# Attention of the last two chunks with keys by halves of a block, and their loads issued elsewhere

## The chip, the cores and the metric

The kernel runs on one core of a Trainium2 chip. The metric is the device time of one execution in microseconds. A core has five engines with a queue each, which work in order: TensorE (PE in the profile; its weight loads are PEld), VectorE (DVE), ScalarE (ACT), GpSimd (POOL) and SyncE (SP), which only issues DMAs here. GpSimd issues DMAs too (those that cast on the way), and all DMAs share 16 DMA engines.

## The reference, cut to what matters

Linear attention with decay, in blocks, and then a feed-forward layer with a PReLU (the reference walks in blocks of 64 positions; the kernel takes 128, which gives the same sums):

```python
q, k, v: (4, 8, 768, 64) fp32       # batch, heads, positions, head_dim
rel   = pos[:, None] - pos[None, :]
Dmask = where(rel >= 0, lam ** rel, 0)
for each block:
    intra = ((qb @ kb.T) * Dmask) @ vb
    inter = (qb * lam ** (pos + 1)) @ kv_state
    out   = intra + inter
    kv_state = lam ** block * kv_state + (kb * lam ** (block - 1 - pos)).T @ vb
x = out as (3072, 512)
h = x @ w_in                        # (512, 2048)
g = max(h, 0) + alpha * min(h, 0)
result = g @ w_out                  # (2048, 512), fp32
```

Within a block only the pairs with key position at or before the query position count; the mask is zero for the others.

## The kernel before

**Units and chunks.** The kernel takes blocks of L = 128 positions and windows of W = 256 (two blocks, numbered a = 0 and 1). A chunk c is one window of two of the four batch entries; there are six chunks, and the window of chunk c is c // 2. Each chunk is cut into four units by batch entry (bi) and half of the heads (hh), so unit n is chunk n // 4; units 16 to 23 are the last two chunks, 4 and 5. For these two chunks' window only the state of the first of its blocks is still needed, so their state products number 8 instead of 16.

**Positions.** Loads put neighbouring positions beside each other in one partition: partition p of a window holds positions 2p and 2p + 1 (e = 0 and 1), 128 numbers in a row, 512 bytes in HBM. Block a lies in partitions 64a to 64a + 63. A block's 128 keys are thus cut into even and odd ones.

**One unit's way.** `load` (L80) brings q, k and v in fp32, from SyncE by default; `load_v16` (L274) brings v from GpSimd and casts it on the way. `cast` (L263) makes fp16 copies of q and k in one tile `qk16`. `transposes` (L306) turns this tile by a DMA transpose from SyncE into `qkT`. `key_decayed` (L287) multiplies k by its decay (tile `kdec`) and `decayed` (L350) the turned q by its decay (tile `qdT`), nearly always on GpSimd. Then come the matmuls:

- `inter` (L368): decayed queries times state R, 128 columns, into the accumulator `acc`.
- `score_products` (L384): 16 matmuls of 64x64 quadrants, 128 query columns each, for two head pairs (hp) x two key halves (e) x four quadrants, into PSUM tile `s`.
- `masked` (L399): VectorE multiplies `s` (128 x 1024) by `dmask` into `sm`.
- `intra` (L409): 16 quadrant matmuls of values times `sm`, 128 columns each, into `acc`.
- `state_products` (L429): quadrant matmuls of `kdec` and values, 64 columns each, into the other half of `acc`; `states` (L455) folds them into R on VectorE.
- `attended` (L445): ScalarE copies `acc` into the chunk's `xT`.

`cluster(old, new)` (L478) issues these for two units at once, in this order on TensorE: inter of the old unit, scores of the new one, intra of the old one, state products of the new one. So the masked multiply of a unit has the time until the next cluster.

**The feed-forward layer.** `up(c, f, ...)` (L540) makes four matmuls of 512 columns into a bank of PSUM, ScalarE a negated relu `m` (L553) and VectorE the activation `g` (L560) from it. `down(c, t, part, ...)` (L567) multiplies four of the 16 tiles of `g` by `w_out`. For the chunks from 3 on, `down2` (L695) does this with sums of quarter matrices (`product`, L642; `g_sum`, L627; `weight_sum`, L615).

**The order.** Nothing is scheduled automatically. The order of each engine's queue is the order of the calls: up to L1037 a list written out by hand, and from L1045 a table `plan` for chunks 3, 4 and 5, whose entries are called at numbered steps of an alternation of up and down products. While chunk c's up products run, the clusters of chunk c + 1 come between. [...] The pools set how many tiles of a kind live at once: `raw` five, `qk16` four, `qkT` three, `v16` and `kdec` eight each (a unit's v is one tile).

## Time and profile before

| | us |
|---|---|
| median of 3 runs | 207.44 (207.35 to 207.44) |
| the profiled execution, its own time | 207.43 |
| its span, first to last instruction | 205.7 |
| TensorE busy | 200.0 (97%) |
| VectorE busy | 159.7 (78%) |
| ScalarE busy | 113.6 (55%) |
| GpSimd busy | 110.0 (53%) |

The span leaves out what lies around the program's instructions, 1.7 us here. The mean granted clock of TensorE is 0.997 of full speed. In the profile's rows, a timeline row gives start, duration, engine, line, operation, what it writes and reads, its shape and how many such instructions were merged; in brackets stands the idle time of that engine before it and what ended it. A row of a group gives the same by line and shape with the count, the busy time and the mean in ns.

### The profile page before, as it was taken

To read this page: it belongs to the slowest core of one execution; us is meant where nothing else is said; L and a number is where in the kernel's file an instruction comes from. 1 tells how busy PE (TensorE), PEld (TensorE's weight loads), DVE (VectorE), ACT (ScalarE), POOL (GpSimd) and SP (SyncE) were. 2 spreads that over 40 slices of the span, in tenths; PEclk is the share of its full clock that TensorE was granted. 3 is DMA by queue.
4 is the path that set the end of the run, shared out by engine and by line. 5 is a ranking of instruction groups with operands and counts; after the bars stand their busy time and mean duration, and the time that the engine had idled before them with its cause. 6 is when DMAs were issued, how large, how long until landed. Compare 5 with 4: busy or idle time off the path is not lost.

```text
span 205.7 us, 5585 instructions
## 1 busy us (share of the span) xinstructions
PE 200.0 (97%) x2271; PEld 122.7 (60%) x2271; DVE 159.7 (78%) x289; ACT 113.6 (55%) x210; POOL 110.0 (53%) x132
## 2 busy tenths in 40 slices
PE   7999999999999999999999999999999999999992
PEld 6976445556445455555555455466666666666882
DVE  6978879568888847899998887959999467675921
ACT  7885778144786217656776466653553544444320
POOL 8999794053577883295346995562094040552000
PEclk9999999999999999999999999999999999999998
DMA  5999999997999995999989974540001111011223
GB/s 165 278 197 234 245 259 207 233 285 238 222 266 233 207 292 131 242 155 137 175 100 269 203 201 78 77 102 21 33 0 54 64 42 51 2 51 54 81 73 105
DMA packets 58206, 31.18 MB, mean 152 GB/s; under 512 B 27124, under 2 KB 55940, under 8 KB 58180
## 3 DMA queue, kind: packets, MB, share of 16 engines
q1 hardware_dynamic: 42740, 21.12, 42.3%
q0 software_dynamic: 15136, 9.57, 29.3%
q8 instruction: 18, 0.29, 0.6%
q10 hardware_dynamic: 304, 0.13, 0.2%
q14 instruction: 8, 0.07, 0.1%
HBM read 27.27 MB, written 6.29 MB: 163 GB/s over the span
## 4 chain that ended last, share of the span: by engine, by line
PE 92%; DVE 2%; ACT 2%; issue 1%; ACTq 0%; DVEq 0%
PE h_ps L545 40%; PE o_ps L573 21%; PE o_ps L655 16%; PE s L391 4%; PE acc L416 3%; PE unread L152 2%; PE acc L375 2%; PE tpx L341 2%; PE acc L436 1%; DVE g L638 1%; ACT L180 1%; ACT m L553 1%; ACT xT L250 1%; DVE sm L402 1%; PE p L655 0%
## 5 line engine op out<-in xcount | busy, mean ns | idle before, releaser
L545 PE MATMUL h_ps<-xT,w_in_sb 128*128 128x512 f16 (+1 forms) x392 | 91.9, 375 | 0.2 <-DVE g L560 0.2
L560 DVE SCALAR_TENSOR_TENSOR g<-m,oma,h_ps 128x512 f16<-128x512 f32 (+1 forms) x98 | 71.1, 734 | 25.1 <-ACT m L553 22.0
L553 ACT ACTIVATE m<-h_ps 128x512 f32<-128x512 f32 (+1 forms) x98 | 57.3, 588 | 46.6 <-PE h_ps L545 40.4
L545 PEld LDWEIGHTS <-w_in_sb 128*128 128x128 f16 x392 | 37.5, 98 | 37.4 <-issue 0.4
L573 PE MATMUL o_ps<-w_out_sb,g 128*128 128x512 f16 x192 | 46.8, 380 | 0.0
L402 DVE TENSOR_TENSOR sm<-s,dmask 128x1024 f16<-128x1024 f32 x24 | 29.2, 1218 | 10.8 <-PE s L391 10.7
L655 PEld LDWEIGHTS <-g 128*128 128x128 f16 x296 | 28.2, 98 | 8.2
L638 POOL TENSOR_TENSOR s<-g 128x512 f16<-128x512 f16 x11 | 12.8, 1163 | 32.6 <-PE o_ps L655 16.7
L573 PEld LDWEIGHTS <-g 128*128 128x128 f16 x192 | 17.7, 98 | 19.4 <-DVE g L560 0.2
L250 ACT ACTIVATE xT<-acc 128x512 f16<-128x512 f32 x24 | 14.3, 597 | 24.3 <-PE acc L436 22.2
L355 POOL TENSOR_TENSOR qdT<-qkT,qdecay 128x512 f16<-128x512 f16 (+1 forms) x19 | 21.1, 1116 | 8.5 <-DMA qkT<-qk 5.3
L655 PE MATMUL o_ps<-w_out_sb,g 128*128 128x256 f16 x192 | 24.1, 273 | 0.0
L291 POOL TENSOR_TENSOR kdec<-kraw,kdecay 128x512 f16<-128x512 f32 x18 | 19.2, 1069 | 6.5 <-DVE g L560 5.4
L254 POOL CAST qk<-qraw 128x512 f16<-128x512 f32 x12 | 7.7, 645 | 18.2 <-DMA qraw<-in_q_dram 18.2
L465 DVE SCALAR_TENSOR_TENSOR R<-R,rdecay,acc 128x128 f16<-128x128 f16 x54 | 15.4, 338 | 0.0
L278 POOL DMA_DIRECT2D v<-in_v_dram x19 | 14.9, 790 | 0.4 <-issue 0.4
L638 POOL TENSOR_TENSOR g<-g 128x512 f16<-128x512 f16 x11 | 13.3, 1206 | 0.9
L687 ACT ACTIVATE o_sb<-o_ps 128x512 f32<-128x512 f32 (+1 forms) x15 | 7.5, 497 | 7.6 <-PE o_ps L655 7.6
L655 PE MATMUL o_ps<-w_sum,g 128*128 128x256 f16 x88 | 11.3, 273 | 0.0
L391 PE MATMUL s<-qkT 64*64 64x128 f16 x384 | 10.1, 221 | 0.0
L416 PE MATMUL acc<-sm,v 64*64 64x128 f16 x384 | 9.8, 218 | 0.1
L690 DVE TENSOR_TENSOR o_sb<-o_sb,o_ps 128x512 f32<-128x512 f32 (+1 forms) x12 | 6.5, 548 | 4.2 <-PE o_ps L655 2.2
(84 smaller groups left out, 194.5 us busy)
## 6 DMA issues: line engine op xcount, KB each, us to landing
out_dram<-o_sb SPq DMA_DIRECT2D x20, 256.0 KB, 2.6
kraw<-in_k_dram SPq DMA_DIRECT2D x7, 512.0 KB, 5.4
qraw<-in_q_dram SPq DMA_DIRECT2D x6, 512.0 KB, 5.5
v<-in_v_dram POOLq DMA_DIRECT2D x19, 128.0 KB, 5.7
w_in_sb<-in_moe_w_in_dram POOLq DMA_DIRECT2D x4, 512.0 KB, 8.5
w_out_sb<-in_moe_w_out_dram POOLq DMA_DIRECT2D x4, 512.0 KB, 10.5
qraw<-in_q_dram POOLq DMA_DIRECT2D x6, 256.0 KB, 7.2
qraw<-in_q_dram SPq DMA_DIRECT2D x6, 256.0 KB, 4.8
```

The costliest lines, as they stand in the source:

```text
L250: nc.scalar.activation(out, in_, AF.Copy)
L291: engine(eng).tensor_tensor(out=kdec, in0=kr, in1=kdecay[:, ds(4 * hh, 4), :].rearrange("p h e -> p e h").unsqueeze(3).to_broadcast([128, ...
L355: engine(eng).tensor_tensor(out=qdT[:, :, :, p], in0=(t["qps"] if eng == "P" else t["qkT"][:, 0])[:, :, :, p], in1=qdecay[:, hh, :, :, p], ...
L391: nc.tensor.matmul(t["s"][ds(a * 64, 64), hl, hp, 1 - e, :].rearrange("p (e j) -> p e j", e=2), lhsT=t["qkT"][p, 1, e, hp, ds(a * 64, 64)] ...
L402: nc.vector.tensor_tensor(out=t["sm"].rearrange("p a h x j -> p (a h) x j"), in0=t["s"].rearrange("p a h x j -> p (a h) x j"), in1=mask_of ...
L416: nc.tensor.matmul(ot[a][ds(hl * 64, 64), hp, :], lhsT=t["v16"][p, 2 * hp + hl, e, :], rhs=t["sm"][p, hl, hp, 1 - e, :], start=(2 * pb + a ...
L545: nc.tensor.matmul(h_ps[:, 0:n] if bi is None else h_ps[:, 0:n].rearrange("p (e j) -> p e j", e=2), lhsT=w_in_sb[:, gi, ts(f, 128)], rhs=x ...
L553: nc.scalar.activation(m[:, 0:n], h_ps[:, 0:n], AF.Relu, scale=-1.0)
L560: nc.vector.scalar_tensor_tensor(out=g, in0=mv, scalar=oma[:, f : f + 1], in1=hv, op0=ALU.mult, op1=ALU.add)
L573: nc.tensor.matmul(o_ps, lhsT=lhs(c, f, t), rhs=w_out_sb[:, f, :], start=(f == 0), stop=(f == NF - 1),)
L638: engine(eng).tensor_tensor(out=out, in0=in0, in1=in1, op=op)
L655: nc.tensor.matmul(t[:, cols], lhsT=x, rhs=w, start=(fresh and f == 0), stop=(last and f == NF // 2 - 1), skip_group_check=True,)
```

## The change

For units 16 to 23 the 128 keys of a block are cut into the first and the last 64 positions instead of even and odd ones. The queries keep their even and odd order. The last 64 keys meet only the last 64 queries, so that the second half's score matmuls and intra matmuls have 64 columns, and the masked multiply reads 192 of each 256 score columns. What follows from it:

- k of these chunks is loaded by four DMAs of 64 partitions and 256-byte runs in place of one with 512-byte runs (`load`), v by four casting DMAs for both units of a half chunk in place of two (`load_vh`, two issues a call; a tile of v now holds both units).
- A second key decay `hdecay` for the new positions (`half_positions` on GpSimd, `half_key_decay` on ScalarE).
- A second mask, in a free raw tile for the first half of the heads and in place of the first mask for the second: four SyncE transfers each (`half_mask`) and a copy on GpSimd for the later keys (`later_half`).
- Calls that move: k of (4, 0) from before the last q and v loads of chunk 3 to after the transpose of unit 13; q and k of (5, 0) from behind the transpose of unit 18 to ahead of it, q first; k and q of (5, 1) to after the transpose of unit 19; v of chunk 5 out of `prepared` to steps 5, 22 and 30 of the plan. v of chunk 4 is issued at the four places at which its units were issued before.

The diff, cut where only context stood:

```diff
@@ -44,11 +44,13 @@
     DFF = moe_w_in.shape[1]
     NF = DFF // 128
     CH = 2 * W
+    HC = NC - 2
 
     const = ctx.enter_context(tc.tile_pool(name="const", bufs=1))
     raw_pool = ctx.enter_context(tc.tile_pool(name="raw", bufs=5))
     half_pool = ctx.enter_context(tc.tile_pool(name="half", bufs=4))
     kv_pool = ctx.enter_context(tc.tile_pool(name="kvh", bufs=8))
+    v_pool = ctx.enter_context(tc.tile_pool(name="vh", bufs=4))
     qkt_pool = ctx.enter_context(tc.tile_pool(name="qkt", bufs=3))
     sm_pool = ctx.enter_context(tc.tile_pool(name="sm", bufs=2))
     xt_pool = ctx.enter_context(tc.tile_pool(name="xt", bufs=2))
@@ -86,6 +88,14 @@
             raws[c, bi][x] = raw_pool.tile([128, H, 2 * D], fp32, tag=f"{x}raw", name=f"{x}raw")
         heads = ds(0, H) if half is None else ds(4 * half, 4)
         i = "kqv".index(x)
+        if x == "k" and c >= HC:
+            for a in range(2):
+                for f in range(2):
+                    nc.sync.dma_start(
+                        out=raws[c, bi][x][ds(64 * a, 64), heads, ds(D * f, D)],
+                        in_=k[b, heads, ds(pb * W + L * a + 64 * f, 64), :].rearrange("h p d -> p h d"),
+                    )
+            return
         (nc.gpsimd if queue == "G" else nc.sync).dma_start(
             out=raws[c, bi][x][:, heads, :],
             in_=(k, q, v)[i][b, heads, ds(pb * W, W), :].rearrange("h (p e) d -> p h (e d)", e=2),
@@ -218,6 +228,44 @@
         for e in range(2):
             nc.scalar.activation(kdecay[:, :, e], loglam, AF.Exp, scale=rev_f[:, e : e + 1])
 
+    hdecay = const.tile([128, H, 2], fp32, name="hdecay")
+    rev_h = const.tile([128, 2], fp32, name="rev_h")
+
+    def half_positions():
+        for half in range(2):
+            nc.gpsimd.iota(
+                rev_i[ds(half * 64, 64)], pattern=[[-64, 2]], base=L - 1, channel_multiplier=-1
+            )
+        nc.gpsimd.tensor_copy(out=rev_h, in_=rev_i)
+
+    def half_key_decay():
+        for f in range(2):
+            nc.scalar.activation(hdecay[:, :, f], loglam, AF.Exp, scale=rev_h[:, f : f + 1])
+
+    HM = {}
+
+    def half_mask(hh):
+
+        m = [dmask[:, x].rearrange("p l h a j -> p (l h) (a j)") for x in range(2)]
+        if hh == 0:
+            t = raw_pool.tile([128, H, 2 * D], fp32, tag="vraw", name="hmask")
+            HM[0] = t.rearrange("p h d -> p (h d)")[:, 0:768].rearrange("p (x j) -> p x j", j=192)
+        else:
+            HM[1] = m[0]
+        for a in range(2):
+            for e in range(2):
+                nc.sync.dma_start(
+                    out=HM[hh][64 * a + e : 64 * a + 64 : 2, :, 0:L],
+                    in_=m[hh][ds(64 * a, 32), :, ds(64 * (1 - e), L)],
+                )
+
+    def later_half(hh):
+
+        nc.gpsimd.tensor_copy(
+            out=HM[hh][:, :, L:192].rearrange("p x (e j) -> p x e j", e=2),
+            in_=HM[hh][:, :, 0:L].rearrange("p x (e j) -> p x e j", e=2)[:, :, :, 0:32],
+        )
+
     llp = const.tile([128, NHP], fp32, name="llp")
     nc.vector.tensor_copy(out=llp[0:64, :], in_=llv[0:64, 0, :])
     nc.vector.tensor_copy(out=llp[64:128, :], in_=llv[64:128, 1, :])
@@ -263,7 +311,7 @@
     def cast(n, name, eng):
         t = T.setdefault(n, {})
         if name == "v16":
-            t[name] = kv_pool.tile([128, 4, 2, D], fp16, tag=name, name=name)
+            t[name] = v_of(n)
             c, bi, hh = units[n]
             copy_on(eng, t[name].rearrange("p h e d -> p h (e d)"), raws[c, bi]["v"][:, ds(4 * hh, 4), :])
             return
@@ -271,10 +319,28 @@
             t["qk16"] = half_pool.tile([128, 2, 2, 4, D], fp16, tag="qk16", name="qk16")
         copy_on(eng, t["qk16"][:, int(name == "k16")], raw_of(n)[name])
 
+    V = {}
+
+    def v_of(n):
+        c, bi, hh = units[n]
+        if (c, bi) not in V:
+            V[c, bi] = v_pool.tile([128, H, 2, D], fp16, tag="v16", name="v16")
+        return V[c, bi][:, ds(4 * hh, 4)]
+
+    def load_vh(c, bi, a):
+
+        for n in (4 * c + 2 * bi, 4 * c + 2 * bi + 1):
+            T.setdefault(n, {})["v16"] = v_of(n)
+        for f in range(2):
+            nc.gpsimd.dma_start(
+                out=V[c, bi][ds(64 * a, 64), :, f],
+                in_=v[2 * (c % 2) + bi, :, ds((c // 2) * W + L * a + 64 * f, 64), :].rearrange("h p d -> p h d"),
+            )
+
     def load_v16(n):
 
         c, bi, hh = units[n]
-        v16 = kv_pool.tile([128, 4, 2, D], fp16, tag="v16", name="v16")
+        v16 = v_of(n)
         nc.gpsimd.dma_start(
             out=v16.rearrange("p h e d -> p h (e d)"),
             in_=v[2 * (c % 2) + bi, ds(4 * hh, 4), ds((c // 2) * W, W), :].rearrange("h (p e) d -> p h (e d)", e=2),
@@ -287,11 +353,12 @@
     def key_decayed(n, eng="G"):
         hh = units[n][2]
         kr = raw_of(n)["k16"]
+        decay = hdecay if units[n][0] >= HC else kdecay
         kdec = kv_pool.tile([128, 2, 4, D], fp16, tag="kdec", name="kdec")
         engine(eng).tensor_tensor(
             out=kdec,
             in0=kr,
-            in1=kdecay[:, ds(4 * hh, 4), :].rearrange("p h e -> p e h").unsqueeze(3).to_broadcast([128, 2, 4, D]),
+            in1=decay[:, ds(4 * hh, 4), :].rearrange("p h e -> p e h").unsqueeze(3).to_broadcast([128, 2, 4, D]),
             op=ALU.mult,
         )
         T.setdefault(n, {})["kdec"] = kdec
@@ -384,6 +451,20 @@
     def score_products(n):
         t = T[n]
         t["s"] = ps.tile([128, 2, 2, 2, L], fp32, tag="s", name="s")
+        if units[n][0] >= HC:
+            s = t["s"].rearrange("p l h x j -> p l h (x j)")
+            for hp in range(2):
+                for f in range(2):
+                    for a, hl in QUADS:
+                        p = ds(hl * 64, 64)
+                        nc.tensor.matmul(
+                            s[ds(a * 64, 64), hl, hp, ds(L * f, L - 64 * f)].rearrange("p (e j) -> p e j", e=2),
+                            lhsT=t["qkT"][p, 1, f, hp, ds(a * 64, 64)],
+                            rhs=t["qkT"][p, 0, :, hp, ds(a * 64 + 32 * f, 64 - 32 * f)],
+                            start=True,
+                            stop=True,
+                        )
+            return
         for hp in range(2):
             for e in range(2):
                 for a, hl in QUADS:
@@ -399,6 +480,10 @@
     def masked(n):
         t = T[n]
         t["sm"] = sm_pool.tile([128, 2, 2, 2, L], fp16, tag="sm", name="sm")
+        if units[n][0] >= HC:
+            out, in0 = (y.rearrange("p a h x j -> p (a h) (x j)")[:, :, 0:192] for y in (t["sm"], t["s"]))
+            nc.vector.tensor_tensor(out=out, in0=in0, in1=HM[units[n][2]], op=ALU.mult)
+            return
         nc.vector.tensor_tensor(
             out=t["sm"].rearrange("p a h x j -> p (a h) x j"),
             in0=t["s"].rearrange("p a h x j -> p (a h) x j"),
@@ -413,10 +498,15 @@
             for e in range(2):
                 for hl, a in QUADS:
                     p = ds(a * 64, 64)
+                    o, x = ot[a][ds(hl * 64, 64), hp, :], t["sm"][p, hl, hp, 1 - e, :]
+                    if units[n][0] >= HC:
+                        o = o.rearrange("p (e j) -> p e j", e=2)[:, :, ds(32 * e, 64 - 32 * e)]
+                        x = t["sm"][p, hl, hp].rearrange("p x j -> p (x j)")[:, ds(L * e, L - 64 * e)]
+                        x = x.rearrange("p (e j) -> p e j", e=2)
                     nc.tensor.matmul(
-                        ot[a][ds(hl * 64, 64), hp, :],
+                        o,
                         lhsT=t["v16"][p, 2 * hp + hl, e, :],
-                        rhs=t["sm"][p, hl, hp, 1 - e, :],
+                        rhs=x,
                         start=(2 * pb + a == 0 and hp == 0 and e == 0),
                         stop=(e == 1),
                         skip_group_check=True,
@@ -927,6 +1017,7 @@
     up(1, 1, None, "op")
     cast(11, "k16", "G")
     query_decay(3, 0)
+    half_positions()
     up(1, 2, None, "h")
     load_v16(10)
     up(1, 12, None, "tk")
@@ -968,11 +1059,11 @@
     cluster(9, 10, "A")
     cast(16, "q16", "G")
     down(1, 3, 0, 4, "op")
+    half_key_decay()
     down(1, 0, 2, 4, "tk")
     transposes(12, "D", False)
     key_decayed(12, "G")
     decayed(12, "G")
-    load(4, 0, "k", None)
     load(3, 1, "q", 1)
     down(1, 3, 1, 4, "op")
     cluster(10, 11, "A")
@@ -981,6 +1072,7 @@
     down(1, 2, 2, 4, "h")
     cast(12, "v16", "A")
     transposes(13, "D", False)
+    load(4, 0, "k", None)
     cast(15, "v16", "G")
     cast(14, "k16", "A")
     cast(14, "v16", "G")
@@ -989,9 +1081,10 @@
     transposes(14, "D", False)
     down(1, 2, 3, 4, "h")
     load(4, 0, "q", 1)
+    half_mask(0)
     cast(15, "k16", "G")
     cast(17, "q16", "G")
-    load_v16(19)
+    load_vh(4, 0, 0)
     cluster(11, 12, "A")
     down(1, 0, 3, 4, "tk")
     transposes(15, "D", False)
@@ -999,7 +1092,7 @@
     up(2, 14, None, "tk")
     decayed(13, "V")
     up(2, 5, None, "h")
-    load_v16(16)
+    load_vh(4, 0, 1)
     key_decayed(17, "G")
     up(2, 2, None, "h")
     up(2, 0, None, "tk")
@@ -1007,20 +1100,22 @@
     cast(17, "k16", "G")
     decayed(14, "G")
     cast(16, "k16", "G")
-    load_v16(17)
+    load_vh(4, 1, 0)
     cluster(12, 13, "A")
     transposes(16, "D", False)
     down(1, 3, 2, 4, "op")
     up(2, 1, None, "h")
-    load_v16(18)
+    load_vh(4, 1, 1)
     up(2, 15, None, "h")
     load(4, 1, "k", None)
     up(2, 8, None, "tk")
     decayed(15, "G")
     key_decayed(16, "G")
     key_decayed(18, "G")
+    later_half(0)
     cluster(13, 14, "A")
     down(1, 3, 3, 4, "op")
+    half_mask(1)
     up(2, 10, None, "h")
     up(2, 13, None, "h")
     up(2, 11, None, "op")
@@ -1029,10 +1124,13 @@
     up(2, 3, None, "tk")
     up(2, 6, None, "h")
     up(2, 9, None, "op")
+    later_half(1)
     decayed(16, "G")
     cluster(15, 16, "A")
     up(2, 7, None, "tk")
     transposes(17, "D", False)
+    load(5, 0, "q")
+    load(5, 0, "k")
     cast(18, "q16", "A")
     cast(18, "k16", "A")
 
@@ -1044,20 +1142,23 @@
 
     plan = {
         3: {
-            0: lambda: (turned(18), load(5, 0, "k"), load(5, 0, "q"), decayed(17)),
+            0: lambda: (turned(18), decayed(17)),
             2: lambda: prepared(19),
+            5: lambda: (load_vh(5, 0, 0), load_vh(5, 0, 1)),
             4: lambda: cluster(16, 17),
-            7: lambda: (turned(19), decayed(18)),
+            7: lambda: (turned(19), decayed(18), load(5, 1, "k"), load(5, 1, "q")),
             10: lambda: prepared(20),
             11: lambda: cluster(17, 18),
-            13: lambda: (turned(20), decayed(19), load(5, 1, "k"), load(5, 1, "q")),
+            13: lambda: (turned(20), decayed(19)),
             17: lambda: prepared(21),
             18: lambda: cluster(18, 19),
             20: lambda: (turned(21), decayed(20)),
+            22: lambda: (load_vh(5, 1, 0)),
             24: lambda: prepared(22),
             26: lambda: cluster(19, 20),
             28: lambda: (turned(22), decayed(21)),
             29: lambda: prepared(23),
+            30: lambda: (load_vh(5, 1, 1)),
         },
         4: {
             0: lambda: (turned(23), decayed(22)),
```

## The prediction

> **What bounds the kernel now.** I read the page's busy times and its chain first, then the order of time on TensorE around a chunk boundary, then VectorE, GpSimd and SyncE in the same stretch.
>
> ```profile
> PE 200.0 (97%) x2271; PEld 122.7 (60%) x2271; DVE 159.7 (78%) x289; ACT 113.6 (55%) x210; POOL 110.0 (53%) x132
> ...
> PE 92%; DVE 2%; ACT 2%; issue 1%; ACTq 0%; DVEq 0%
> ```
>
> TensorE is busy for 200.0 of 205.7 us and holds 92% of the chain. Time therefore falls only if TensorE streams less, and any wait of TensorE is paid in full. The order of time shows how dense it is (start, duration, then the operation):
>
> ```profile
> 100.68 1.90 PE L545 MATMUL h_ps<-xT,w_in_sb 128*128 128x512 f16 x8
> 102.42 1.03 PE L573 MATMUL o_ps<-w_out_sb,g 128*128 128x512 f16 x4
> 103.28 1.03 PE L545 MATMUL h_ps<-xT,w_in_sb 128*128 128x512 f16 x4
> 104.15 1.03 PE L573 MATMUL o_ps<-w_out_sb,g 128*128 128x512 f16 x4
> 105.01 0.39 PE L375 MATMUL acc<-qdT,R 128*128 128x128 f16 x4
> ...
> 145.08 1.02 PE L545 MATMUL h_ps<-xT,w_in_sb 128*128 128x512 f16 x4 [0.21 <-DVE g L560]
> ```
>
> Four 512-column matmuls start every 0.86 to 0.87 us (102.42 to 103.28 to 104.15), 0.216 us each, with nothing between. The only gap in the stretch that the change touches is the 0.21 us before 145.08, where TensorE waited for VectorE.
>
> **What it removes on TensorE.** In the eight units 16 to 23, half of the score matmuls and half of the intra matmuls go from 128 to 64 moving columns. Whether that saves anything is read from the quadrant matmuls of one cluster (unit 11 enters, unit 10 leaves): first those into the output accumulator (128 columns), then the state products (64 columns). The count in brackets is how many were in flight within the window; since nothing of the group had started earlier, it counts starts.
>
> ```profile
> 80.59:80.61 0.02, 0.01 (x4) 1.00 0.00 0
> 80.59:80.76 0.17, 0.16 (x12) 1.00 0.00 0
> 80.59:80.78 0.19, 0.18 (x16) 1.00 0.00 0
> ```
>
> ```profile
> 80.81:80.84 0.03, 0.02 (x4) 1.00 0.00 0
> 80.81:80.91 0.10, 0.09 (x12) 1.00 0.00 0
> 80.81:80.93 0.12, 0.11 (x16) 1.00 0.00 0
> ```
>
> Both start in groups of four, one for each quadrant. At 128 columns the fourth group starts between 80.76 and 80.78, about 0.165 us after the first: 55 ns a group. At 64 columns it is about 0.09 us after: 30 ns a group. A halved group saves 25 ns. Each unit has two such groups in its scores and two in its intra products: 8 x 4 x 25 ns = 0.80 us. Bounds: nothing, if alternating 128 and 64 columns kept the slower pace, and 0.80. I take 0.80, because both rows are quadrant groups of the same shape.
>
> **What it removes on VectorE.** The masked multiply reads 768 instead of 1024 columns:
>
> ```profile
> L402 DVE TENSOR_TENSOR sm<-s,dmask 128x1024 f16<-128x1024 f32 x24 | 29.2, 1218 | 10.8 <-PE s L391 10.7
> ...
> L690 DVE TENSOR_TENSOR o_sb<-o_sb,o_ps 128x512 f32<-128x512 f32 x6 | 4.1, 678 | 0.0
> ...
> L690 DVE TENSOR_TENSOR o_sb<-o_sb,o_ps 128x256 f32<-128x256 f32 x6 | 2.4, 417 | 4.2 <-PE o_ps L655 2.2 <-ACT o_sb L687 2.0
> ```
>
> The additions from PSUM cost 678 - 417 = 261 ns for 256 columns, so a multiply goes from 1218 to about 957 ns, 2.1 us over eight. VectorE is off the path except at the gap before 145.08. A multiply lies a few operations ahead of it, so I credit 0.20 us there (bounds 0 and 0.21). The gain without any new wait is 0.80 + 0.20 = 1.00 us.
>
> **What it adds on GpSimd.** Here is its queue before unit 16 enters:
>
> ```profile
> 86.13 0.61 POOL L254 CAST qk<-qraw 128x512 f16<-128x512 f32 x1 [6.11 <-DMA qraw<-in_q_dram]
> 86.69 0.79 POOL L278 DMA_DIRECT2D v<-in_v_dram  x1
> 87.85 0.77 POOL L278 DMA_DIRECT2D v<-in_v_dram  x1 [0.37 <-issue]
> ...
> 91.31 0.60 POOL L254 CAST qk<-kraw 128x512 f16<-128x512 f32 x1
> 91.86 1.55 POOL L278 DMA_DIRECT2D v<-in_v_dram  x2
> 93.42 1.17 POOL L355 TENSOR_TENSOR qdT<-qkT,qdecay 128x512 f16<-128x512 f16 x1
> 94.55 1.05 POOL L291 TENSOR_TENSOR kdec<-kraw,kdecay 128x512 f16<-128x512 f32 x1
> 100.95 1.05 POOL L291 TENSOR_TENSOR kdec<-kraw,kdecay 128x512 f16<-128x512 f32 x1 [5.36 <-DVE g L560]
> 101.96 2.29 POOL L355 TENSOR_TENSOR qdT<-qkT,qdecay 128x512 f16<-128x512 f16 x2
> ```
>
> Everything that the change puts on GpSimd and ScalarE earlier (positions, two small exponentials) ends in the 6.11 us in which GpSimd waits for q before 86.13, and costs nothing. After that it does cost. A value load of one unit was one issue of about 0.78 us; a chunk half now needs four issues for two units. A row's run is halved but the pieces per issue (64 partitions x 8 heads instead of 128 x 4) stay the same, so I keep 0.78. The two issues at 86.69 and 87.85 become four, so the k cast of unit 16 (91.31, ending 91.91) ends 2 x 0.78 = 1.56 us later, at 93.5. The two at 91.86 become four as well: the decayed query of unit 15 then ends near 97.8 and the decayed key of unit 16 near 98.8. TensorE wants them at 99.67 and 100.46 (the cluster before the 100.68 row), so they still fit. Bounds on an issue: if time goes with partitions, 0.39 us and no delay; if with bytes, the same.
>
> **What it moves on SyncE.** The transpose of unit 16 waits for that cast, and the k load of the second chunk half is queued behind it:
>
> ```profile
> 91.94 1.23 SPq L311 DMA_TRANSPOSE qkT<-qk  x1
> 93.22 0.57 SPq L89 DMA_DIRECT2D kraw<-in_k_dram  x1
> ```
>
> ```profile
> kraw<-in_k_dram SPq DMA_DIRECT2D x1, 512.0 KB, 7.7
> ```
>
> Before, k(4,1) left at 93.22 and landed 7.7 us later, at 100.9: just when GpSimd's waiting decayed key (100.95, unit 18) starts. The page names VectorE for that wait, but the landing fits to 0.1 us. Now the transpose leaves at 93.5 instead of 91.94, holds the queue for 1.23, and four issues of 0.57 follow: the last piece is out at 97.0 instead of 93.8. Then the transfer. Three queue rows give the price of a packet (count, MB, share of 16 engines) in windows of 4, 2 and 2 us:
>
> ```profile
> q0 software_dynamic: 957, 0.24, 63.7%
> q1 hardware_dynamic: 512, 0.12, 27.9%
> q1 hardware_dynamic: 1245, 0.61, 116.0%
> ```
>
> A software packet of 256 B (values, 94 to 98 us) costs 0.637 x 4 x 16 / 957 = 42.6 ns of one engine, a hardware packet of 256 B (a transpose, 78 to 80) 17.4, one of 512 B (a load, 66 to 68) 29.8. Before: 1024 x 17.4 (transpose) + 1024 x 29.8 (k) + 1024 x 42.6 (values), over 16 engines, is 5.7 us from 93.2 on; the landing took 7.7, 1.35 times as long. Now k is 2048 packets and the values 2048, of 128 B, for which no row stands. With 17.4 as their floor: 5.6 us, with 42.6 as ceiling 8.8, times 1.35, from 94.7 on: landing at 102.3 to 106.6. If the last piece, out at 97.0, needed only half of the 7.7 us, it would land at 101, and that is my lower end; the upper is 106.6. I take **103.2**, near the lower end, since the bytes are the same and only the packets are smaller.
>
> **Who waits for that landing.** The decayed key of unit 18 stands in GpSimd's queue ahead of the new copy of the later half of mask 0, that ahead of the copy for mask 1, and that ahead of the decayed query of unit 16. The first masked multiply with the new mask (unit 16) now waits for GpSimd, and VectorE is in order:
>
> ```profile
> 101.49 1.22 DVE L402 TENSOR_TENSOR sm<-s,dmask 128x1024 f16<-128x1024 f32 x1
> 102.62 0.59 DVE L465 SCALAR_TENSOR_TENSOR R<-R,rdecay,acc 128x128 f16<-128x128 f16 x2
> 103.14 1.52 DVE L560 SCALAR_TENSOR_TENSOR g<-m,oma,h_ps 128x512 f16<-128x512 f32 x2
> ```
>
> Decayed key: 103.2 + 1.05 = 104.25. Mask copy, 256 columns: the 512-column cast takes 0.61, so 0.3 to 0.6, say 0.45: 104.7. The multiply starts there instead of at 101.49. From its start to the activations at 103.14 were 1.65 us, now 1.39; the first activation, the last tile of chunk 2, takes half of 1.52: done at 104.7 + 1.39 + 0.76 = 106.85. TensorE needs that tile for the fourth matmul of the down product at 104.15, at 104.15 + 3 x 0.216 = 104.80. **Stall: 2.05 us**; in general, the landing minus 101.15. Beside it and not added to it: the decayed query of unit 16 ends at 104.7 + 0.45 + 1.16 = 106.3 against 105.01; the transpose of unit 17 waits for the second k piece and lands near 106 against about 105.3. Both are inside the same stall. Later clusters have more: unit 18 enters at about 112 us. The eight mask transfers fall between transposes whose units enter some 10 us later; if that cover went, each would cost an issue, 0.57 us.
>
> **Sum.** The profiled execution took 207.43 us (span 205.7, 1.7 around it), the median of three is 207.44. 207.43 - 0.80 - 0.20 + 2.05 = **208.5 us**. About 0.2%, 0.4 us, is what a measurement of this kernel can tell from no change. The change breaks even at a stall of 1.0 us, a landing at 102.15.
>
> **Weighed against the skill.** The 512 B packet cost 29.8 ns here and the 256 B one 17.4, so the smaller packet was nearly proportionally cheaper, though that row is a transpose inside SBUF. The Trainium skill ("DMA: Bandwidth & Descriptors", Specifications) says that a transfer under 512 B is not at line rate since it turns into read-modify-write; the trace neither shows nor excludes it for reads of 256 B from HBM. By that rule the halved k rows land later, and the time is that of the second rival below.
>
> **Rivals.** (1) *Hidden.* The landing is at or before 101.15, no one waits, and the time is 207.43 - 1.00 = 206.4. For it: an issue of half the partitions may be cheaper, which gives back 1.56 us on both queues; the 10 us of slack elsewhere. Against: four pieces behind one another and twice the software packets. Decides: landing before about 101.7. (2) *Small packets are as dear as large ones.* A k packet of 256 B costs the 29.8 ns of a 512 B one: 2048 x 12.4 / 16 x 1.35 = 2.1 us more, landing at 105.3, stall 4.15, time 210.6. For it: nothing in the trace prices a 256 B read of HBM; against: the 17.4. (3) *The change does not shorten the matmuls*: mixed groups keep 55 ns; only 0.20 is gained and the stall stays: 209.3. Against it stands the 30 ns of the state products.
>
> **How the numbers follow.** Forecast, partly hidden: 0.47; its own range is 207.0 to 209.7 (landing 101.7 to 104.4), and 0.12 of its chance lies within 0.2% of before. Hidden: 0.28. Dear packets: 0.15. No shorter matmuls: 0.10. So faster 0.28, within 0.12, slower 0.35 + 0.15 + 0.10 = 0.60. The range has to hold the hidden case and most of the dear one: 206.3 to 210.4.
>
> **What would show it.** Right: the score groups' second halves at 30 ns; masked multiplies near 0.96 us; k(4,1) landing after 102 us; a VectorE wait for GpSimd before the multiply of unit 16; one TensorE gap near 105 us of some 2 us, and none elsewhere. Wrong: no gap near 105 us, value issues well under 0.78 us, or the gap at another cluster, most of all at a transpose that lands late.

## The result, and the profile after

| | before | changed |
|---|---|---|
| median, us (20 runs each, in turns) | 207.3 (206.8 to 208.07) | 208.1 (206.75 to 209.97) |
| ratio of times, 95% interval | | 1.0032 (1.0019 to 1.0046) |
| profiled execution, us | 207.43 | 208.76 |
| its span, us | 205.7 | 207.0 |

The changed kernel is slower by 0.2 to 0.5%, some 0.7 us. The forecast was 208.5 us, slower. The ratio leaves out the changed kernel's longest run (209.97 us), which counts as a slow one. The profiled execution took 0.66 us more than the median and is the second longest of the twenty, so that the waits read below are probably shorter in a typical execution.

The page of the profiled execution, busy times and chain of waits:

```profile
PE 200.0 (97%) x2271; PEld 122.6 (59%) x2271; DVE 156.0 (75%) x289; ACT 113.9 (55%) x212; POOL 116.0 (56%) x145
...
PE 87%; DMA 4%; DVE 2%; POOL 1%; ACT 1%; SPq 1%; issue 1%; ACTq 0%; POOLq 0%
```

TensorE's share of the chain falls from 92 to 87%, and DMAs, absent from the chain before, hold 4%. What TensorE waited for (total, times, longest, in us):

```profile
PE o_ps L663 <- DVE g L650: 1.1, 1, 1.1
...
PE s L460 <- DMA qkT<-qk: 0.7, 1, 0.7
```

There are two waits, not one. In the order of time on TensorE (start, duration):

```profile
102.72 1.03 PE L663 MATMUL o_ps<-w_out_sb,g 128*128 128x512 f16 x4
...
104.45 0.81 PE L663 MATMUL o_ps<-w_out_sb,g 128*128 128x512 f16 x3
106.40 0.39 PE L663 MATMUL o_ps<-w_out_sb,g 128*128 128x512 f16 x1 [1.14 <-DVE g L650]
106.63 0.39 PE L442 MATMUL acc<-qdT,R 128*128 128x128 f16 x4
106.94 0.37 PE L460 MATMUL s<-qkT 64*64 64x128 f16 x16
107.14 0.34 PE L506 MATMUL acc<-sm,v 64*64 64x128 f16 x16
107.31 0.29 PE L526 MATMUL acc<-v,kdec 64*64 64x64 f16 x8
...
113.59 0.39 PE L442 MATMUL acc<-qdT,R 128*128 128x128 f16 x4
114.69 0.37 PE L460 MATMUL s<-qkT 64*64 64x128 f16 x16 [0.71 <-DMA qkT<-qk]
...
145.75 1.04 PE L745 MATMUL o_ps<-w_sum,g 128*128 128x256 f16 x8
146.83 1.02 PE L635 MATMUL h_ps<-xT,w_in_sb 128*128 128x512 f16 x4
```

I count waits from start to start, since a matmul's end in a row lies behind the moment at which the next could start. The fourth matmul of the down product (the 106.40 row) could have started at 104.45 + 3 x 0.216 = 105.10 and started at 106.40: **1.30 us** lost. From `inter` (113.59) to the scores it is 0.31 us elsewhere (106.63 to 106.94); at unit 18 it is 1.10: **0.79 us** lost. Before 146.83, eight matmuls of 0.109 from 145.75 on end at 146.62, so 0.2 us is left there.

The halved groups are seen against the same cluster before:

```profile
105.33 0.42 PE L391 MATMUL s<-qkT 64*64 64x128 f16 x16
105.57 0.39 PE L416 MATMUL acc<-sm,v 64*64 64x128 f16 x16
105.80 0.29 PE L436 MATMUL acc<-v,kdec 64*64 64x64 f16 x8
```

Scores to intra was 0.24 and is 0.20, intra to state products was 0.23 and is 0.17: 0.05 us each on the mean, 0.10 a unit, 0.80 over eight. And the masked multiply:

```profile
L485 DVE TENSOR_TENSOR sm<-s,hmask 128x768 f16<-128x768 f32 x4 | 3.8, 954 | 2.3 <-POOL hmask L264 2.3
L485 DVE TENSOR_TENSOR sm<-s,dmask 128x768 f16<-128x768 f32 x4 | 3.8, 950 | 0.0
```

Laying the two traces over each other matmul by matmul, the last matmul comes 1.47 us later: 0.36 was there before any unit of chunk 4 (the two executions differ in their first microseconds), + 1.30, + 0.78, - 0.17 at the gap that was at 145.08, - 0.80 in steps of 0.1 a unit.

**First wait, step by step.** GpSimd, then SyncE, then VectorE, all of the changed kernel:

```profile
86.71 0.61 POOL L302 CAST qk<-qraw 128x512 f16<-128x512 f32 x1 [7.62 <-DMA qraw<-in_q_dram]
87.31 0.73 POOL L335 DMA_DIRECT2D v<-in_v_dram  x1
88.41 2.06 POOL L335 DMA_DIRECT2D v<-in_v_dram  x3 [0.37 <-issue]
...
93.15 0.61 POOL L302 CAST qk<-kraw 128x512 f16<-128x512 f32 x1
93.70 2.75 POOL L335 DMA_DIRECT2D v<-in_v_dram  x4
...
102.79 1.05 POOL L358 TENSOR_TENSOR kdec<-kraw,hdecay 128x512 f16<-128x512 f32 x1 [4.14 <-DMA kraw<-in_k_dram]
103.78 0.40 POOL L264 COPY hmask<-hmask 128x256 f32<-128x256 f32 x1
```

```profile
93.79 1.27 SPq L378 DMA_TRANSPOSE qkT<-qk  x1
95.11 4.26 SPq L94 DMA_DIRECT2D kraw<-in_k_dram  x4
...
104.16 0.57 SPq L99 DMA_DIRECT2D qraw<-in_q_dram  x1
104.77 3.12 SPq L94 DMA_DIRECT2D kraw<-in_k_dram  x4
108.06 4.44 SPq L378 DMA_TRANSPOSE qkT<-qk  x2
```

```profile
104.21 0.96 DVE L485 TENSOR_TENSOR sm<-s,hmask 128x768 f16<-128x768 f32 x1 [2.29 <-POOL hmask L264]
...
105.60 1.40 DVE L650 SCALAR_TENSOR_TENSOR g<-m,oma,h_ps 128x512 f16<-128x512 f32 x2
```

The cast of unit 16's k ends at 93.76, the transpose that waits for it leaves at 93.79, the k pieces follow from 95.11 on. The decayed key that needs the last piece starts at 102.79 after 4.14 us of idle time, the mask copy at 103.78, the multiply at 104.21, the activations 1.39 us behind it. From the first issue of k of (4, 1) to the decayed key it took 7.7 us here (95.11 to 102.79) and 7.7 us before (93.22 to 100.95): the key came 1.84 us later because the issue came 1.89 us later, and the split into four pieces of smaller packets shows no effect on top of that.

**Second wait.** The transpose of unit 18, the first of the two at 108.06, leaves after q and the four pieces of k of (5, 0), which occupy SyncE from 104.16 on. Before, it left at 103.47, those loads after it, and the decayed query that needs it had it by 108.05:

```profile
108.05 1.16 POOL L355 TENSOR_TENSOR qdT<-qkT,qdecay 128x512 f16<-128x512 f16 x1 [2.80 <-DMA qkT<-qk]
```

Now the scores that need it wait until 114.69.

### The profile page after: what moved, and what is told of

Its sections match the earlier page's. It is cut to its first block, busy times and chain, and to the rows that moved or that the text cites. A ratio compares the mean times of both kernels' runs of the same rounds, so it can differ in the third digit from the quotient of the medians.

```text
span 207.0 us, 5639 instructions
## 1 busy us (share of the span) xinstructions
PE 200.0 (97%) x2271; PEld 122.6 (59%) x2271; DVE 156.0 (75%) x289; ACT 113.9 (55%) x212; POOL 116.0 (56%) x145
## 4 chain that ended last, share of the span: by engine, by line
PE 87%; DMA 4%; DVE 2%; POOL 1%; ACT 1%; SPq 1%; issue 1%; ACTq 0%; POOLq 0%
PE h_ps L635 36%; PE o_ps L663 19%; PE o_ps L745 17%; DMA qkT<-qk 3%; PE unread L162 3%; PE s L472 2%; PE acc L506 2%; PE tpx L408 2%; PE acc L442 2%; POOL qdT L422 1%; DVE g L650 1%; DMA dmask<-dmask 1%; PE acc L526 1%; PE s L460 1%; SPq L257 1%
## 5 line engine op out<-in xcount | busy, mean ns | idle before, releaser
L635 PEld LDWEIGHTS <-w_in_sb 128*128 128x128 f16 x392 | 37.5, 98 | 37.2 <-issue 0.2
L487 DVE TENSOR_TENSOR sm<-s,dmask 128x1024 f16<-128x1024 f32 x16 | 19.5, 1222 | 11.4 <-PE s L472 11.4
L358 POOL TENSOR_TENSOR kdec<-kraw,hdecay 128x512 f16<-128x512 f32 x8 | 9.0, 1122 | 4.1 <-DMA kraw<-in_k_dram 4.1
L335 POOL DMA_DIRECT2D v<-in_v_dram x16 | 11.1, 701 | 0.4 <-issue 0.4
L358 POOL TENSOR_TENSOR kdec<-kraw,kdecay 128x512 f16<-128x512 f32 x10 | 10.5, 1056 | 0.9 <-DMA kraw<-in_k_dram 0.9
L302 POOL CAST qk<-kraw 128x512 f16<-128x512 f32 x9 | 5.5, 615 | 8.8 <-DMA kraw<-in_k_dram 8.8
```

Source lines behind the costliest of these rows:

```text
L302: nc.gpsimd.tensor_copy(out=out, in_=in_)
L358: engine(eng).tensor_tensor(out=kdec, in0=kr, in1=decay[:, ds(4 * hh, 4), :].rearrange("p h e -> p e h").unsqueeze(3).to_broadcast([128, 2 ...
L487: nc.vector.tensor_tensor(out=t["sm"].rearrange("p a h x j -> p (a h) x j"), in0=t["s"].rearrange("p a h x j -> p (a h) x j"), in1=mask_of ...
L635: nc.tensor.matmul(h_ps[:, 0:n] if bi is None else h_ps[:, 0:n].rearrange("p (e j) -> p e j", e=2), lhsT=w_in_sb[:, gi, ts(f, 128)], rhs=x ...
```

## Experiments

The theory: the change is worth 1.0 us by itself; GpSimd's additional value issues delay the k cast of unit 16, hence transpose, k(4, 1), decayed key, mask copy and multiply, hence the first wait; and the second wait comes from the move of the (5, 0) loads. The rival for the first: the smaller k packets are dear. The rival for the second: the small packets of the values slow the transpose down. Each kernel was compared with the kernel before on the same chip (medians 207.23 to 207.28).

### The gain alone

Kernel before, with the matmuls and the multiply cut to 64 and 192 columns for units 16 to 23 by the same slices as in the change, and none of its loads, masks and decays. The core of the edit, in scores, multiply and intra:

```diff
-                        rhs=t["qkT"][p, 0, :, hp, ds(a * 64, 64)],
+                        rhs=t["qkT"][p, 0, :, hp, ds(a * 64 + 32 * f, 64 - 32 * f)],
...
+            out, in0 = (y.rearrange("p a h x j -> p (a h) (x j)")[:, :, 0:192] for y in (t["sm"], t["s"]))
...
+                        o = o.rearrange("p (e j) -> p e j", e=2)[:, :, ds(32 * e, 64 - 32 * e)]
```

> The kernel before, with only the computing part of the change: in units 16 to 23 half of the score and intra matmuls have 64 columns and the masked multiply reads 768 columns. It leaves out the sums of the even keys with the other queries and takes a mask of the wrong places; no load, mask transfer or copy is added or moved. Theory (the gain is 0.80 us of TensorE streaming and about 0.2 us at the one gap before 145 us, all the rest is waits): 1.0 us less than before, a ratio of 0.995, no gap near 105 or 114 us. Rival (mixed groups of 64 and 128 columns keep the slow pace, or VectorE or another engine takes the gain back): within 0.2 us of before.

Measured: 206.35 us, ratio 0.995 (0.9932 to 0.9968), about 1.0 us less, and no wait of TensorE near 105 or 114 us. The gain of 1.00 us is there (0.93 by the medians).

### The k cast ahead of the value issues

```diff
     cast(17, "q16", "G")
+    cast(16, "k16", "G")
     load_vh(4, 0, 0)
...
-    cast(16, "k16", "G")
```

> The changed kernel with one move: GpSimd's cast of k of unit 16 goes ahead of the first four value issues, so that the transpose of unit 16 and behind it the k pieces of (4, 1) leave SyncE earlier. Theory (the k pieces land late because GpSimd's extra value issues hold up that cast): pieces leave from about 91 us instead of 95.1, GpSimd's decayed key of unit 18 no longer waits (it starts at about 98.5 instead of 102.8), the first gap goes, and with SyncE ahead of time the second one mostly too: 206.3 to 206.8, a ratio to before of 0.995 to 0.998. Rival (small packets: twice the number of value and k packets share the engines, so the landing moves little): decayed key not before 101.5, first gap at least 0.5 us.

Measured: **205.98** us (205.63 to 206.07), ratio 0.9938 (0.9916 to 0.996). Of its GpSimd and VectorE:

```profile
100.75 1.05 POOL L358 TENSOR_TENSOR kdec<-kraw,hdecay 128x512 f16<-128x512 f32 x1 [3.05 <-DMA kraw<-in_k_dram]
```

```profile
102.17 0.96 DVE L485 TENSOR_TENSOR sm<-s,hmask 128x768 f16<-128x768 f32 x1 [0.51 <-POOL hmask L264]
```

The decayed key comes 2.04 us earlier than in the changed kernel (0.56 of it because q landed earlier in this execution, 86.15 against 86.71), though not by the 98.5 that I had expected, and the time is 0.3 us below the expected range; the multiply still waits 0.51 us, which TensorE does not feel. Both waits of TensorE are gone, the second too, since the transpose of unit 18 also leaves 2.00 us earlier (106.06). One moved line turns 0.3% slower into 0.6% faster. Reordering alone restores the time, without a change of any packet: TensorE's last group starts at 199.96, against 199.95 with the short products alone and 202.31 in the changed kernel.

### Fewer value issues

```diff
     def load_vh(c, bi, a):
+        if c == 4:
+            nc.gpsimd.dma_start(
+                out=V[c, bi][:, ds(4 * a, 4)].rearrange("p h e d -> p h (e d)"),
+                in_=v[2 * (c % 2) + bi, ds(4 * a, 4), ds((c // 2) * W, W), :].rearrange("h (p e) d -> p h (e d)", e=2),
+            )
+            return
```

> The changed kernel with the values of chunk 4 loaded as before the change, two issues of 128 partitions and 512-byte runs per chunk half in place of four; the values then lie at the wrong positions. Theory (the k pieces of (4, 1) land late because two extra issues of 0.69 us hold up the cast of unit 16): the cast ends 1.4 us earlier than in the changed kernel, the k pieces land at about 101, the decayed key of unit 18 starts 1.4 to 2 us earlier, the first gap falls under 0.3 us and the time to 206.6 to 207.4. Rival (the landing is late for the four k pieces and their small packets alone): the decayed key starts less than 0.7 us earlier, first gap at least 0.7 us.

Measured: 206.59 us, ratio 0.9967 (0.9949 to 0.9985).

```profile
91.16 0.60 POOL L302 CAST qk<-kraw 128x512 f16<-128x512 f32 x1
...
101.30 1.05 POOL L364 TENSOR_TENSOR kdec<-kraw,hdecay 128x512 f16<-128x512 f32 x1 [5.86 <-DMA kraw<-in_k_dram]
```

The cast starts 1.99 us earlier (0.73 of it because q landed earlier in this execution) and the decayed key 1.49 us; the first wait falls to 0.22 us and the second to 0.07. This also halves the count of value packets, so by itself it does not separate issues from packets; the reordering above does.

### k of (4, 1) in one transfer

```diff
-        if x == "k" and c >= HC:
+        if x == "k" and c >= HC and (c, bi) != (4, 1):
```

> The changed kernel with k of (4, 1) loaded as before the change, one transfer with 512-byte runs in place of four with 256-byte runs; the keys of units 18 and 19 then lie at the wrong positions. Theory (the lateness comes from the delayed cast, and 256-byte packets at 20 ns cost about what half as many 512-byte ones cost at 29): landing at most 1 us earlier than in the changed kernel, first gap 0.3 to 1.3 us, time 207.2 to 208. Rival (small or split k transfers are dear): landing 2 us or more earlier, first gap gone, time below 207.2.

Measured: 207.42 us, ratio 0.9994 (0.997 to 1.0018). The profiled execution took 209.08 us, 1.66 more than that median. SyncE, GpSimd and TensorE:

```profile
94.66 0.63 SPq L99 DMA_DIRECT2D kraw<-in_k_dram  x1
```

```profile
103.90 1.05 POOL L358 TENSOR_TENSOR kdec<-kraw,hdecay 128x512 f16<-128x512 f32 x1 [5.72 <-DMA kraw<-in_k_dram]
```

```profile
101.11 0.37 PE L460 MATMUL s<-qkT 64*64 64x128 f16 x16 [1.06 <-DMA qkT<-qk]
```

One issue, 512-byte runs, out 0.45 us before the first of the four pieces, and the decayed key came 1.1 us later than with four pieces: the dear-packet rival expected the reverse. The median is within what the theory expected, the first wait of this execution (1.64 us from start to start) is above its 1.3. The execution is no clean test, though: with three issues fewer ahead of them the mask transfers started at 96.08 instead of 100.14, in the middle of this transfer, and TensorE already waited 1.06 us for the transpose of unit 16. The price of a packet points the same way. Packets, MB and share of 16 engines, first of the changed kernel from 98.5 to 100 us, then of this one from 98 to 100 us:

```profile
q1 hardware_dynamic: 1069, 0.27, 84.5%
q0 software_dynamic: 572, 0.07, 76.3%
```

```profile
q1 hardware_dynamic: 600, 0.31, 70.4%
```

A 256 B read cost 0.845 x 1.5 x 16 / 1069 = 19.0 ns, one of 512 B 0.704 x 2 x 16 / 600 = 37.5 ns in the same crowd (29.8 in the emptier window of the prediction), and a software packet of 128 B 32.0 ns. Packet times overlap (the first two rows add up to 161% of 16 engines), so these figures say how long a packet took and not how much of an engine it used up. They also depend on the window: from 97 to 99.5 us the changed kernel's hardware packets took 22.1 ns (923, 50.9%), from 95 to 97 us, transposes among them, 24.3 ns (943, 71.7%). So a 256 B packet took less than one of 512 B, between half and four fifths of it. The Trainium skill ("DMA: Bandwidth & Descriptors", Specifications) has transfers under 512 B below line rate through read-modify-write; 19.0 against 37.5 ns shows no such loss for these reads into SBUF, 24.3 against 29.8 would be one, so the rows do not settle it.

### The loads of (5, 0) behind the transpose again

```diff
-    load(5, 0, "q")
-    load(5, 0, "k")
...
-            0: lambda: (turned(18), decayed(17)),
+            0: lambda: (turned(18), load(5, 0, "k"), load(5, 0, "q"), decayed(17)),
```

> The changed kernel with one move: the q and k loads of (5, 0) go back behind the transpose of unit 18. Theory (the second gap, 0.7 to 0.9 us at the scores of unit 18, comes from this transpose standing in SyncE's queue and in the transfer queue behind five loads): that gap goes, the first one at 105 to 106 us stays at 1.1 to 1.3 us, time 0.8 us below the changed kernel, 207.1 to 207.4, about equal to before. Rival (the transpose is late because everything on SyncE ahead of it is late, the k pieces of (4, 1) and the mask transfers, and the five loads only follow): the gap shrinks by less than half.

Measured: 208.06 us, ratio 1.0052 (1.003 to 1.0074): a miss. The wait at the scores of unit 18 is gone, but q of (5, 0) now comes last behind four issues of k, and ScalarE, in order, waits with its cast; behind it stands the relu that `up` needs:

```profile
116.11 0.63 ACT L298 ACTIVATE qk<-qraw 128x512 f16<-128x512 f32 x1 [3.30 <-DMA qraw<-in_q_dram]
```

```profile
118.06 1.02 PE L635 MATMUL h_ps<-xT,w_in_sb 128*128 128x512 f16 x4 [1.16 <-DVE g L650]
```

The wait moved on by 4 us and grew. SyncE has five issues where it had two; with the queue as late as this, whichever of the transpose and the loads stands last is late.

### The value issues of (5, 0) later

```diff
-            5: lambda: (load_vh(5, 0, 0), load_vh(5, 0, 1)),
+            15: lambda: (load_vh(5, 0, 0), load_vh(5, 0, 1)),
```

> The changed kernel with one move: the four value issues of (5, 0) go from step 5 to step 15 of the plan, behind the cluster in which unit 18 enters. Theory A (the transpose of unit 18 lands late because its packets share the engines with these software packets): the second gap at the scores of unit 18 goes, the first stays at 1.1 to 1.4 us, time 207.1 to 207.4. Theory B (the transpose lands late because of the q and k loads ahead of it on SyncE and in its own queue): the second gap stays at 0.7 us or more, time about as the changed kernel.

Measured: 208.07 us, ratio 1.0048 (1.0026 to 1.0071). The second wait did not appear, but only because the first was longer (1.70 + 0.22 us, the decayed key only at 103.61 in code that up to there is the changed kernel's), so TensorE came late to unit 18. The transpose itself was hardly earlier than in the changed kernel. It left SyncE at 108.05 (108.06 there), and the decayed query that waited for it started here:

```profile
114.58 1.16 POOL L422 TENSOR_TENSOR qdT<-qkT,qdecay 128x512 f16<-128x512 f16 x1 [4.67 <-DMA qkT<-qk]
```

In the changed kernel that was 114.81. Without the value packets beside it, the transpose took 6.5 us instead of 6.75, which speaks against the rival. Later value loads also cost 0.24 and 0.67 us at 145 to 147 us.

### The mask copy ahead of the decayed keys

```diff
+    later_half(0)
     key_decayed(16, "G")
     key_decayed(18, "G")
-    later_half(0)
```

> The changed kernel with one move: the copy for mask 0 goes ahead of the decayed keys of units 16 and 18 on GpSimd. Theory (VectorE's multiply of unit 16 waits for that copy and for nothing else): the multiply starts about 101.8 us again, without a wait for GpSimd, and the gap in the middle of the down product goes; a gap of 0.9 to 1.1 us shows instead at the inter matmuls of unit 16, which wait for the decayed query of unit 16 behind the decayed key of unit 18 and the copy for mask 1. So the time falls by 0.2 to 0.4 us only. Rival (the cluster's own inputs, a late transpose of unit 17, set the gap): the gap does not get smaller and stands at the scores of unit 17.

Measured once: 212.56 us. The multiply starts at 102.00 without a wait and the first wait is 0.25 us, less than the 0.9 to 1.1 expected. Yet the time rose: TensorE arrives earlier at unit 18, whose transpose does not.

```profile
112.69 0.39 PE L442 MATMUL acc<-qdT,R 128*128 128x128 f16 x4
115.52 0.37 PE L460 MATMUL s<-qkT 64*64 64x128 f16 x16 [2.45 <-DMA qkT<-qk]
...
116.22 1.89 PE L663 MATMUL o_ps<-w_out_sb,g 128*128 128x512 f16 x4
```

```profile
116.50:119.00 2.50, 2.50 (x7) 0.91 (x6) 1.01 (x3) 0.42 (x1) 2.50 (x4) 0.50 1.06 187
```

The last row is a window's length and its busy time by engine (TensorE first); behind the last bracket stand the granted clock, 0.50, the DMA share and GB/s. After the wait TensorE ran at half clock until about 119.3 us. From the scores to the ninth matmul of 512 columns took 3.96 us (115.52 to 119.48), against 2.33 in the next execution of the same kernel (113.53 to 115.86): 1.6 us more on top of 2.5. The Trainium skill ("TensorE: Matmul & The Clock Gate", Part 1) has the half clock come after an idle window of about 3.4 us whose phase runs freely; here some 2.5 us of waiting, with one short product in front, was enough. This execution's span is 5.1 us longer than that of the next one; the other 2.4 us lie elsewhere, 0.9 of them before unit 16 and 1.5 behind the last matmul.

The same kernel again, with more runs:

> The kernel with the copy for mask 0 ahead, a second time and timed, since its single run took 212.56 us with a gap of 2.6 us at the scores of unit 18 and a clock of 0.986. Theory (the first gap shrinks by nearly 1 us, and the gap at unit 18 varies from run to run with the transfers): median 207.3 to 208.3, with single runs above 209.5 when that gap exceeds 2.5 us and the clock falls. Rival (this order makes the gap at unit 18 larger for good): median above 210.

Measured: 207.51 us (206.9 to 209.79), ratio 1.0009 (0.9983 to 1.0034). In this profile:

```profile
113.53 0.37 PE L460 MATMUL s<-qkT 64*64 64x128 f16 x16 [1.36 <-DMA qkT<-qk]
```

The first wait is 0.27 us, 1.03 less than in the changed kernel, and the second, from start to start, 1.44, 0.65 more (the 1.53 of the next expectations has 0.09 of the usual step in it). So two thirds of what the mask copy gave back at 105 us was taken at unit 18: the second wait was partly covered by the first. The longest of the twelve runs, 209.79 us, has a mean granted clock of 0.990, the others 0.997 or more, so the half clock may have come in that one too; it has no trace.

### What makes the transpose of unit 18 late

With the mask copy ahead, TensorE should come on time, and the two explanations of the second wait can be told apart: value issues moved (first kernel), or loads moved back (second), by the edits shown above.

> Two edits on the changed kernel: the mask copy ahead of the decayed keys (which makes the first gap 0.25 us) and the value issues of (5, 0) from step 5 to step 15, away from the transpose of unit 18. With the copy ahead alone, TensorE waited 1.53 us at the scores of unit 18 and the median was 207.51. Theory A (the 128-byte value packets slow the transpose of unit 18 down): that wait shrinks below 0.3 us, median 206.3 to 206.8, unless the later value loads are missed at 145 to 147 us, where the same edit alone showed gaps of 0.24 and 0.67 us; then up to 207.3. Theory B (the five issues of q and k of (5, 0) ahead in SyncE's queue alone make the transpose late): the wait stays at 1.2 to 1.8 us, median 207.3 to 207.9.

Measured: 207.75 us, ratio 1.0024 (1.0008 to 1.004). The profile did not have TensorE on time:

```profile
105.25 0.40 POOL L264 COPY dmask<-dmask 128x256 f32<-128x256 f32 x1 [1.31 <-DVE w_sum L711]
...
113.06 1.17 POOL L422 TENSOR_TENSOR qdT<-qkT,qdecay 128x512 f16<-128x512 f16 x1 [4.17 <-DMA qkT<-qk]
```

```profile
106.82 0.38 PE L442 MATMUL acc<-qdT,R 128*128 128x128 f16 x4 [1.76 <-POOL qdT L422]
```

Here the copy for mask 1 starts only at 105.25 and holds up the decayed query of unit 16 (the page names VectorE; the last mask transfer landed at 105.05, which fits to 0.2 us): 1.9 us lost there, none at unit 18. What can be read is the transit of the transpose: issued 107.38, used at 113.06, 5.7 us, against 106.67 to 113.53, 6.9 us, with the value issues in place. That the value packets make this difference is not shown: the transit was 6.5 us with the value issues moved alone (above), and 5.7 us in the last kernel below, which has them in place (105.46 to 111.11). Had TensorE come at 112.1, as with the mask copy alone, it would in any case still have waited 1.0 us.

> Two edits on the changed kernel: the mask copy ahead of the decayed keys, and the transpose of unit 18 ahead of q and k of (5, 0) again, as in the kernel before. Theory B (the loads ahead in the queue): the wait of TensorE at the scores of unit 18 goes (below 0.3 us). What then remains is the wait of ScalarE for q of (5, 0), which alone gave TensorE gaps of 1.32 and 0.31 us at the up products after 116 us; here TensorE arrives there 1.1 us earlier, so 1.5 to 2.5 us, median 207.3 to 208.2. Theory A (the value packets): the wait at the scores of unit 18 stays above 0.8 us.

Measured: 207.44 us (206.16 to 209.05), ratio 1.0014 (0.9992 to 1.0036). ScalarE and TensorE of the profile, which is the fastest of the twelve runs:

```profile
113.17 0.63 ACT L298 ACTIVATE qk<-qraw 128x512 f16<-128x512 f32 x1 [1.74 <-DMA qraw<-in_q_dram]
```

```profile
112.16 0.37 PE L460 MATMUL s<-qkT 64*64 64x128 f16 x16
```

The scores of unit 18 start without a wait with the value issues in place, so the order of SyncE's queue is enough to make the second wait and to take it away. ScalarE's wait for q of (5, 0) cost TensorE only 0.08 us in this execution, not the 1.5 to 2.5 expected. The median lies 1.3 us above it; what the other executions lost is not seen.

### Both first-wait edits

The k cast ahead of the value issues and the mask copy ahead of the decayed keys.

> The candidate for the best version: the k cast of unit 16 ahead of the four value issues (205.98 alone, multiply of unit 16 then at 102.17, 0.51 us late but within slack), and the mask copy ahead of the decayed keys as well. Theory (slack already covers the 0.51 us): the same time, 205.8 to 206.1, the multiply's 0.51 us wait gone from VectorE, no TensorE gap over 0.25 us. Rival (the copy waits for its mask transfers, and GpSimd in order holds up the decayed keys behind it): later decayed keys, a gap at inter or state products of units 16 to 18, 206.2 to 207.

Measured: 206.23 us (205.57 to 206.48), ratio 0.9951 (0.9937 to 0.9964); no wait of TensorE above 0.21 us between 95 and 150 us. VectorE's multiply of unit 16, and GpSimd's decayed query of unit 18, which waits for the transpose:

```profile
101.40 0.95 DVE L485 TENSOR_TENSOR sm<-s,hmask 128x768 f16<-128x768 f32 x1
...
111.11 1.16 POOL L422 TENSOR_TENSOR qdT<-qkT,qdecay 128x512 f16<-128x512 f16 x1 [1.88 <-DMA qkT<-qk]
```

The 0.51 us wait of the multiply is gone and the time is no better; the median lies a little over the range, and the intervals of the two kernels overlap. The simpler one, the cast alone (205.98), is the best version found.

## Why the prediction was right, and where it was wrong

- **The gain, 0.80 + 0.20.** Measured 0.80 + 0.17 in the trace, and 1.0 us with the short products alone. The rival of unshortened matmuls falls; so does "hidden", since the first wait was there.
- **The issue, 0.78 us.** The changed kernel's took 0.69 to 0.73. The four before 90.47 took 3.16 us where two had taken 1.93: 1.23 instead of 1.56 us more. The cast still ended at 93.76, later than the forecast's 93.5, because q landed 0.58 us later (86.71 against 86.13), which I had not foreseen; 0.36 of it is the start that the two executions differ by.
- **The landing, 103.2.** By the start of the decayed key, 102.79. The choice near the lower end was right, its way there only in part, so the hit is partly luck. The last piece left SyncE at 99.37 and not at 97.0, since four issues took 4.26 us instead of 4 x 0.57 (the fourth alone 2.08), and it landed 3.4 us behind that. The 7.7 us from first issue to landing stayed as they were before, with the same bytes in twice the packets. The dear-packet rival falls by that and by the reordering; the price of 19.0 to 24.3 ns is below the 29.8 that it assumed, and above the 17.4 of the forecast's floor.
- **The rule, landing minus 101.15.** It gives 102.79 - 101.15 = 1.64; TensorE came 0.30 us later to the down product (102.72 against 102.42), which leaves 1.34, and 1.30 was measured. The 2.05 was 0.75 too high: 0.41 from the landing, 0.30 from TensorE's own lateness, 0.05 from the copy (0.40, not 0.45).
- **One gap "near 105 us of some 2 us, and none elsewhere".** Wrong, and this is the step that failed: "Later clusters have more: unit 18 enters at about 112 us." I counted slack from the chunk boundary and did not follow the transpose of unit 18 through SyncE's queue, where the change put one q and four k issues ahead of it, 3.7 us, on a queue already late. It left 108.06, and its transit was some 6.6 us. The prediction had named this very sign of being wrong, a gap "at a transpose that lands late", but gave it no price. The 0.79 us nearly equals what the first wait fell short by (0.75), so that the forecast's total, 208.5 against 208.1 measured and 208.76 in the profile, came out better than its parts is luck.
- **What one profile cannot tell.** The first wait was 1.30, 1.39 and 1.70 us in three kernels that are the same up to there, as the decayed key came at 102.79, 102.42 and 103.61. A wait that ends with a transfer varied from execution to execution. Whether the changed kernel's times are also more spread out for it is open: without its longest run they lie within 2.0 us, as those of the kernel before did in its 35 runs beside the later experiments (206.86 to 208.88). The two kernels with the cast ahead spread over 0.44 and 0.91 us, but in six runs each. Half clock is not what makes the changed kernel's longest run: its mean granted clock was 0.997, and no run of the twenty was below that, against 0.986 in the execution of 212.56 us.

## What to carry to other kernels

Splitting a transfer to save arithmetic costs issues, and issues are paid by whatever stands behind them in that queue: walk each queue from the split to the next operation that a dense engine needs, for every later unit and not for the first alone. Put the short operation that releases a chain (here a 0.6 us cast) ahead of issues that nobody waits for; that one line made the difference between 0.3% slower and 0.6% faster than before. Taking away a first wait uncovers the second, so test both together.

## What the runs showed of the hardware

- Half clock came once after a wait of about 2.5 us and lasted some 3 us (granted clock 0.50, four matmuls of 512 columns in 1.68 us instead of 0.86); waits of 1.3 to 1.9 us in other kernels kept the full clock.
- A 256 B packet of a read from HBM took 19.0 to 24.3 ns of one of the DMA engines, depending on the window, a 128 B casting packet from GpSimd 32.0 ns, so casting packets, not hardware ones, were the dear ones: half the bytes of the prediction's 256 B casting packet (42.6 ns) for three quarters of its price.
- A transpose in the crowd was slow to issue: 1.27 us at 93.79 in the changed kernel, but 4.44 for two at 108.06 (3.04 of it the first), while loads ahead of it were still in flight.
